# Attention with head mixing, then a leaky MLP: second mixing on array quarters, with a fixed order on every engine

## The chip, the cores and the metric

The kernel runs on one core of a Trainium2 chip. The metric is the time on the device in microseconds, as the median of several runs. TensorE (PE) multiplies matrices into PSUM; VectorE (DVE) and ScalarE (ACT) empty PSUM and work elementwise; GpSimd (POOL) works on SBUF alone; SyncE (SP) issues nearly all transfers.

## The reference

Four batches, twelve heads, 448 positions, head size 64. The scores of the twelve heads are mixed with one another before the softmax (first mixing) and after it (second mixing). The MLP has 1,792 tokens, width 768 and hidden width 2,048.

```python
scores = scale * np.matmul(q, k.transpose(0, 1, 3, 2))
scores = np.einsum('bhij,hg->bgij', scores, w_pre)       # first mixing
scores = scores - np.max(scores, axis=-1, keepdims=True)
attn = np.exp(scores)
attn = attn / (np.sum(attn, axis=-1, keepdims=True) + 1e-09)
attn = np.einsum('bhij,hg->bgij', attn, w_post)          # second mixing
attn_out = np.matmul(attn, v)
x = attn_out.transpose(0, 2, 1, 3).reshape(B * S, H * D)
h = x @ w_in
return np.maximum(0.01 * h, h) @ w_out
```

## The kernel before

The attention goes through the query rows in chunks: 120, 120, 120 and 88 rows of each batch, 16 chunks in all (`NCK`). The work of a chunk falls into three **units** (index `s`), each of up to 40 query rows (two "quads" of 20 rows, index `u`). A chunk of 88 rows is padded to 100, so its last unit has one quad. There are 48 units, and a full one makes four tiles of exponentials.

`scores(n, a)` multiplies q and k for head pair `a` of chunk `n` into two PSUM banks `pss` of pool `ps_x`; ScalarE or VectorE scales them into `st` (rows of the chunk on partitions). `regroup` is a transfer that collects ten rows of all twelve heads, 120 partitions, into a tile `r`. `softmax(n, s, u)` does the first mixing: eight 64x64 products of `r` and the constant `kpre` into two banks `psm` (pools `ps_m`). VectorE then takes the row maxima (`stat`), ScalarE the exponentials (`et`) with their sums, and after a unit's last quad VectorE makes `kp`, the weights of the second mixing divided by the sums. `mix(n, s, c)` does the second mixing for 128 keys `c`: here `et` is the stationary operand, `kp` the moving one, so the result `psa` (pool `ps_a`, two buffers of one bank) has the keys on partitions. It is copied to `at`, or to `half` for the last 64 keys. `values` multiplies `at` with `vt` (and `half` with `vend`) into `psx`, which shares the pool `ps_x` with the scores, and VectorE copies the result to `xo`, which is stored.

Beside this the MLP's weights are narrowed from 64-bit floats in 64 pieces: `Narrow` loads a piece (`craw`), `spread` casts it on ScalarE (`z`, `w`), `assemble` has three operations on VectorE (`top`, `exp`), `join` two on GpSimd and a store. In the last two chunks `prep_x` begins to prepare the attention's output for the MLP: sums of blocks, then each block as a high and a low part (`xh` by ScalarE, `xl` by VectorE).

The order of most matmuls is that of the program (`pin`); most copies, reductions and transfers before the change are placed by a scheduler. The loop has steps: in each chunk twelve of them (`SLOTS`), in every step one `mix`, in some a `softmax` of the next unit and a pair of `scores` of one of the next two chunks. `values` follows a unit's last `mix`. The MLP behind it is not touched.

Of the kernel before, what the change touches and what calls it, by code (L numbers as in the profile page):

```python
# [24 lines left out]
RUN = 2  # L25
# [8 lines left out]
def kernel(  # L34
# [50 lines left out]
    class Narrow:  # L85
# [7 lines left out]
        def __init__(self, pool, f, j, w=None):  # L93
            at = slice(PIECE * j, PIECE * (j + 1))
            self.pool, self.w, self.dst = pool, w, w_dram[f][:, at]
            self.raw = pool.tile([P, PIECE, 2], U32, tag="raw", name="craw", bufs=4)
            nc.sync.dma_start(self.raw.rearrange("p n w -> p (n w)"), w_moe[f, :, at].bitcast(U32))

        def spread(self, pin=lambda ins: ins):
# [3 lines left out]
            self.z = self.pool.tile([P, PIECE], F32, tag="z", name="z")  # L103
# [15 lines left out]
        def join(self, pin=lambda ins: ins):  # L119
# [3 lines left out]
            nc.sync.dma_start(self.dst, w)  # L123
# [11 lines left out]
    ps_a = pool("ps_a", 2, space=PSUM)  # L135
# [17 lines left out]
    def load_k(b, a):  # L153
        t = k_t[b, a] = p_k.tile([P, S], F32, tag="k", name="kt")
        for e in range(2):
            up = slice(D * e, D * (e + 1))
            nc.sync.dma_start(t[up], k[b, up, 2 * a + e, :])
# [4 lines left out]
    def load_q(n, *queues):  # L162
# [3 lines left out]
        for e in range(2):  # L166
            up = slice(D * e, D * (e + 1))
            (queues or (nc.sync, nc.sync))[e].dma_start(t[up, :, :m], src[up, :, e])
# [7 lines left out]
    def load_v(b, s):  # L176
        t = p_v.tile([P, NJ - 1, RUN, 2, D], F32, tag=f"v{s}", name=f"vt{s}")
        at = 2 * RUN * s
        nc.sync.dma_start(t.rearrange("p c a e d -> p c (a e) d"), v[b][:, :NJ - 1, at:at + 2 * RUN])
        for e in range(2):  # L180
            up = slice(HP * e, HP * (e + 1))
            nc.sync.dma_start(v_end[up, RUN * s:RUN * (s + 1), e], v[b][up, NJ - 1, at + e:at + 2 * RUN:2])
        v_t[b, s] = t

    def scores(n, a, banks=(ps_x, "x")):
        b, m = chunks[n][0], width(n)
# [9 lines left out]
        for e, ps in enumerate(two):  # L196
            to = s_t[n][:m, 2 * a + e, :]
            if e and (a % 2 or not n):
                nc.vector.tensor_scalar_mul(to, ps[:m, :S], scale)
            else:  # L200
                nc.scalar.activation(to, ps[:m, :S], AF.Copy, scale=scale)  # L201

    last_dma = [None]
# [4 lines left out]
    def regroup(n, a, z, *queues):  # L208
        m = width(n)
        for g in range(a, min(z, m // ROWS)):  # L210
            r_t[n, g] = t = r_all[turn[0] % SLOTS]
            turn[0] += 1
            last_dma[0] = (queues or (nc.sync, nc.sync))[g % 2].dma_start(
                t[LOW:LOW + RH], s_t[n][g:m:m // ROWS]
            )

    def softmax(n, s, u):
# [12 lines left out]
        for y, ps in enumerate(banks):  # L230
            g = 2 * u + y
            e = p_e.tile([P, S], F32, tag="e", name="et")
            es.append(e)
            nc.vector.tensor_reduce(st[:, 0, g:g + 1], ps[:, :S], axis=AX.X, op=ALU.max, negate=True)  # L234
            nc.scalar.activation(  # L235
                e, ps[:, :S], AF.Exp, bias=st[:, 0, g:g + 1], accum_out=st[:, 1, g:g + 1]
            )
        if u < len(sg) - 1:
            return
        kp = p_st.tile([P, NJ, H, ROWS], F32, tag="kp", name="kp")  # L240
# [3 lines left out]
        nc.vector.tensor_scalar_add(rs, st[:, 1, :z], 1e-9)  # L244
        nc.vector.reciprocal(rs, rs)
        nc.vector.tensor_mul(  # L246
            kp[:, :z].rearrange("p g h x -> p g (h x)"),
            kpost.rearrange("p h x -> p (h x)").unsqueeze(1).broadcast_to([P, z, H * ROWS]),
            rs.unsqueeze(2).broadcast_to([P, z, H * ROWS]),
        )  # L250

    def mix(n, s, c):

        sg = chunks[n][3][s]
        if s == 0 and c == 0:
            at_t[n] = (  # L260
                p_at.tile([P, NJ - 1, H, CHUNK], F32, tag="at", name="at"),
                p_at.tile([P, NPAIR, CHUNK], F32, tag="half", name="half"),
            )
        es, kp = e_t[n, s][0], kp_t[n, s]
        ps = ps_a.tile([P, 512], F32, tag="a", name="psa")
        if c < NJ - 1:
            at, nh, halves = at_t[n][0][:, c], H, ((0, P, 0, 1),)
        else:
            at, nh, halves = at_t[n][1], NPAIR, ((0, HP, 0, 2), (HP, HP, 1, 2))
        w = QUAD * len(sg)  # L270
        to = ps[:, :nh * w].rearrange("p (h u b y r) -> p u y h b r", h=nh, b=2, y=2, r=ROWS // 2)
        for g, e in enumerate(es):
            for p0, np, h, step in halves:
                mm(
                    to[p0:p0 + np, g // 2, g % 2], e[:, c * P:c * P + np],
                    kp[:, g, h::step].rearrange("p h (b r) -> p h b r", b=2), start=True, stop=True,
                )
        copy = nc.scalar.copy if n == NCK - 1 or c % 2 and (s * NJ + c) >= HALF - 1 else nc.vector.tensor_copy
        copy(at[:, :, QUAD * sg[0]:QUAD * sg[0] + w], ps[:, :nh * w].rearrange("p (h w) -> p h w", h=nh))  # L279

    def values(n, s):
        b, m = chunks[n][0], width(n)
        at, half = at_t[n]
# [4 lines left out]
        for a in range(RUN):  # L288
            for c in range(NJ - 1):
                for e in range(2):  # L290
                    mm(
                        ps[D * e:D * (e + 1), a, :m], w[:, c, a, e], at[:, c, 2 * (RUN * s + a) + e, :m],
                        start=a == c == 0, stop=False, skip_group_check=True,
                    )
        for a in range(RUN):
            mm(
                ps[:, a, :m], v_end[:, RUN * s + a].rearrange("p e d -> p (e d)"), half[:, RUN * s + a, :m],
                start=False, stop=a == RUN - 1, skip_group_check=True,
            )
        nc.vector.tensor_copy(  # L300
            xo_t[n][:, RUN * s:RUN * (s + 1), :m].rearrange("p a (x g) -> p a g x", x=ROWS),
            ps[:, :RUN, :m].rearrange("p a (g x) -> p a g x", x=ROWS),
        )
# [591 lines left out]
```

## Time and profile before

| | us |
|---|---|
| median of three runs (876.22 to 882.21) | 876.81 |
| profiled execution, its time | 873.24 |
| profiled execution, its span | 871.5 |
| attention, from the first scores to the first projections of the MLP | about 7 to 458 |

Times within the span are counted from its first instruction. The trace gives two rows for every float32 matmul of the program, and for each a weight load. Durations of consecutive matmuls overlap, so that their pace is read from their starts.

### The profile page before, as it was taken

How to read it: one execution, taken by the hardware profiler on the slowest of the kernel's cores; microseconds unless marked ns; L12 is line 12 of the kernel's file. 1: busy time of each engine (PE TensorE's matmuls, PEld its weight loads, DVE VectorE, ACT ScalarE, POOL GpSimd, SP SyncE). 2: the span in 40 equal slices, each digit the busy share in tenths (PEclk: the TensorE clock that was granted, in tenths of full speed). 3: DMA queues.
4: the chain of work that ended last, by engine and by line, in shares of the span. 5: the costliest groups of instructions: out<-in, count | busy, mean ns of one | idle time of the engine just before them, and what ended most of it. 6: DMA issues, size and time to landing. Idle time of an engine off the chain costs nothing.

```text
span 871.5 us, 17821 instructions
## 1 busy us (share of the span) xinstructions
PE 845.0 (97%) x6712; PEld 669.2 (77%) x6712; DVE 658.4 (76%) x1178; ACT 501.0 (57%) x1044; POOL 136.4 (16%) x154
## 2 busy tenths in 40 slices
PE   7999999999999999999999999999999999999998
PEld 3566666676666666667679999899989999999997
DVE  5688777887778877888897888688797555488565
ACT  2677666666666665666665554455764554454543
POOL 2043333323333232332200000000000000000000
PEclk9999999999999999999999999999999999999999
DMA  7888776997769877585637778536665121133343
GB/s 186 235 255 264 244 231 200 268 253 229 252 201 275 256 241 229 189 259 196 191 93 270 244 252 271 172 109 193 199 206 168 55 64 47 37 107 128 119 128 117
DMA packets 117126, 166.29 MB, mean 191 GB/s; under 512 B 37852, under 2 KB 100656, under 8 KB 117040
## 3 DMA queue, kind: packets, MB, share of 16 engines
q1 hardware_dynamic: 116140, 164.41, 61.2%
q8 instruction: 53, 0.87, 0.4%
q10 hardware_dynamic: 804, 0.73, 0.3%
q14 instruction: 33, 0.27, 0.1%
q0 software_dynamic: 96, 0.01, 0.0%
HBM read 92.91 MB, written 32.64 MB: 144 GB/s over the span
## 4 chain that ended last, share of the span: by engine, by line
PE 66%; DVE 5%; DMA 3%; ACT 2%; issue 1%; SPq 1%; DVEq 0%; ACTq 0%
PE pso L149 38%; PE psa L149 8%; PE psh L149 7%; PE pss L149 5%; PE psx L149 4%; PE psm L149 4%; DMA r<-st 1%; DVE xl L355 1%; DMA qt<-in_q 1%; DMA s_dram<-so 1%; DVE stat L234 1%; ACT et L235 1%; ACT xh L354 1%; DVE xo L300 0%; DVE kp L246 0%
## 5 line engine op out<-in xcount | busy, mean ns | idle before, releaser
L149 PEld LDWEIGHTS psa<-kp,et 128*128 128x128 f32 (+1 forms) x1840 | 157.5, 171 | 71.7 <-ACT st L201 24.0
L149 PE MATMUL psa<-kp,et 128*128 128x120 f32 (+1 forms) x1840 | 177.7, 260 | 3.9 <-DVE kp L246 2.8
L235 ACT ACTIVATE et<-psm,stat 128x448 f32<-128x448 f32 x184 | 115.7, 632 | 69.6 <-DVE stat L234 69.1
L149 PE MATMUL pso<-gh,wl 128*128 128x448 f32 x336 | 123.4, 367 | 1.3 <-ACT gh L354 1.3
L149 PE MATMUL pso<-gl,wh 128*128 128x448 f32 x336 | 123.6, 368 | 0.9 <-DVE gl L355 0.9
L149 PE MATMUL pso<-gh,wh 128*128 128x448 f32 x336 | 123.3, 367 | 0.0
L234 DVE TENSOR_REDUCE stat<-psm 128x1 f32<-128x448 f32 x184 | 106.4, 616 | 17.2 <-PE psm L149 16.9
L149 PE MATMUL pss<-kt,qt 64*64 64x448 f32 (+2 forms) x768 | 104.5, 558 | 6.5 <-DVE xo L300 4.4
L201 ACT ACTIVATE st<-pss 120x448 f32<-120x448 f32 (+1 forms) x141 | 71.9, 544 | 63.0 <-PE pss L149 63.0
L121 POOL TENSOR_TENSOR w<-w,exp 128x384 f32<-128x384 f32 x64 | 65.2, 1018 | 272.5 <-issue 100.0
L149 PE MATMUL psm<-r,kpre 64*64 64x448 f32 (+1 forms) x736 | 99.0, 547 | 6.7 <-DMA r<-st 6.7
L354 ACT CAST wh<-wo 128x768 fp32r<-128x768 f32 x56 | 46.8, 836 | 91.7 <-PE pso L149 86.9
L355 DVE TENSOR_TENSOR wl<-wo,wh 128x768 fp32r<-128x768 f32 x56 | 53.6, 958 | 45.8 <-ACT wh L354 42.2
L279 DVE COPY at<-psa 128x480 f32<-128x480 f32 (+1 forms) x105 | 66.3, 636 | 17.7 <-PE psa L149 17.7
L149 PEld LDWEIGHTS psm<-r,kpre 64*64 64x64 f32 (+1 forms) x736 | 31.9, 135 | 49.4 <-issue 37.0
L149 PEld LDWEIGHTS pso<-gh,wl 128*128 128x128 f32 x336 | 63.6, 189 | 6.7 <-ACT gh L354 1.7
L149 PEld LDWEIGHTS pso<-gl,wh 128*128 128x128 f32 x336 | 63.6, 189 | 6.5 <-DVE gl L355 1.5
L149 PEld LDWEIGHTS pso<-gh,wh 128*128 128x128 f32 x336 | 63.6, 189 | 5.0
L149 PE MATMUL psx<-at,vt 128*64 128x120 f32 (+1 forms) x1152 | 65.4, 263 | 0.5 <-DVE xo L300 0.5
L122 POOL TENSOR_TENSOR w<-w,top 128x384 f32<-128x384 f32 x64 | 64.3, 1004 | 5.0
L355 DVE TENSOR_TENSOR gl<-g,gh 128x896 fp32r<-128x896 f32 x56 | 60.7, 1084 | 1.9 <-ACT gh L354 1.9
L149 PEld LDWEIGHTS psx<-at,vt 128*64 128x64 f32 x1152 | 56.9, 137 | 1.6 <-DVE xo L300 0.7
(117 smaller groups left out, 1415.6 us busy)
## 6 DMA issues: line engine op xcount, KB each, us to landing
r<-st SPq DMA_DIRECT2D x182, 210.0 KB
craw<-in_w_moe SPq DMA_DIRECT2D x64, 384.0 KB
w_dram<-w SPq DMA_DIRECT2D x64, 192.0 KB
wi<-w_dram SPq DMA_DIRECT2D x32, 384.0 KB
wo<-s_dram SPq DMA_DIRECT2D x64, 192.0 KB
wo<-w_dram SPq DMA_DIRECT2D x48, 192.0 KB
xr<-x_dram SPq DMA_DIRECT2D x33, 224.0 KB
so<-w_dram SPq DMA_DIRECT2D x16, 384.0 KB
```

The lines of the kernel that those rows point to most:

```text
L121: pin(nc.gpsimd.tensor_mul(w, w, self.exp.bitcast(F32)))
L122: pin(nc.gpsimd.tensor_add(w, w, self.top.bitcast(F32)))
L149: pin(nc.tensor.matmul(*args, **kw))
L201: nc.scalar.activation(to, ps[:m, :S], AF.Copy, scale=scale)
L234: nc.vector.tensor_reduce(st[:, 0, g:g + 1], ps[:, :S], axis=AX.X, op=ALU.max, negate=True)
L235: nc.scalar.activation(e, ps[:, :S], AF.Exp, bias=st[:, 0, g:g + 1], accum_out=st[:, 1, g:g + 1])
L279: copy(at[:, :, QUAD * sg[0]:QUAD * sg[0] + w], ps[:, :nh * w].rearrange("p (h w) -> p h w", h=nh))
L354: hold(nc.scalar.copy(hi, raw))
L355: hold(nc.vector.tensor_sub(lo, raw, hi.bitcast(F32)))
```

## The change

It rewrites the attention's loop and leaves the MLP's alone.

- The second mixing (`second_mix`) works on 64x64 quarters of the array: 64 rows of `et` (half `b` of the query rows) by 64 keys (half `ch`), with `kp` of 60 columns, or 30 for the last 64 keys. The two row halves go to different banks. A unit's mixing is in two parts of two key blocks each; `ps_a` has one buffer of two banks instead of two of one. One copy empties both banks: VectorE for part 0 (960 elements a partition), ScalarE for part 1 (720). `half` is now a piece of `at`, and `kp` and `kpost` have half the columns.
- Scores are made two chunks ahead: those of chunk `n + 2` in chunk `n`, two pairs in every unit; all pairs of the chunks 0 and 1 come ahead of the loop. The last two chunks have none.
- Every instruction of the attention is pinned to the program's order on its engine, the transfers on SP too. A unit runs: regroup of the next chunk's unit, narrowing load, first mixing of the next unit's quad 0, a score pair, part 0, first mixing of quad 1, a score pair, part 1, `weights` (`kp`), `values` of the chunk before. `join` and `spread` of the narrowing stand at fixed places, a piece in four half units of five (before: one in 8/3 steps, with four steps to a unit).
- Copies out of scores: three of four by ScalarE in every unit. `xo` is copied in two instructions.
- The preparation of x is divided into `join_x` (sums, in the loop on GpSimd) and `split_x`. In the last two chunks part 1 goes through the banks of `ps_x`.

```diff
-    ps_a = pool("ps_a", 2, space=PSUM)
+    ps_a = pool("ps_a", 1, space=PSUM)
...
+    def second_mix(n, s, part, *copies):
         sg = chunks[n][3][s]
...
+        if len(copies) == 1:
+            ps = ps_a.tile([P, 2, 512], F32, tag="a", name="psa")
+            banks = [ps[:, 0], ps[:, 1]]
         else:
...
+            banks = [ps_x.tile([P, 512], F32, tag="x", name="psa") for _ in range(2)]
+        w = ROWS * len(sg)
+        at0 = 0
+        for c in (2 * part, 2 * part + 1):
+            whole = c < NJ - 1
+            nh = H if whole else NPAIR
+            for g, e in enumerate(es):
+                for b in range(2):
+                    for ch in range(2):
+                        up, to = slice(HP * b, HP * (b + 1)), slice(HP * ch, HP * (ch + 1))
+                        keys = slice(c * P + HP * ch * whole, c * P + HP * ch * whole + HP)
+                        out = banks[b][to, at0 * w:(at0 + nh) * w].rearrange(
+                            "p (h g r) -> p g h r", h=nh, r=ROWS // 2
+                        )
+                        weight = kp[up, g] if whole else kp[up, g, ch::2]
+                        mm(out[:, g], e[up, keys], weight, start=True, stop=True)
+            at0 += nh
...
+    for a in range(NPAIR):
+        copy = scores(1, a)
+        copy(0, nc.scalar)
+        copy(1, nc.vector)
...
+        if more:
+            if us > 0:
+                exp = first_mix(*nxt, 0)
+                exp(0)
+            copy = scores(n + 2, 2 * s)
+            copy(0, nc.scalar)
+            if us > 0:
+                exp(1)
+            copy(1, nc.vector)
+            join(2 * i)
+            second_mix(n, s, 0, nc.vector.tensor_copy)
+            spread(2 * i)
+            narrow_load(2 * i + 1)
+            if us > 1:
+                exp = first_mix(*nxt, 1)
+            copy = scores(n + 2, 2 * s + 1)
+            copy(0, nc.scalar)
+            if us > 1:
+                exp(0)
+                exp(1)
+            copy(1, nc.scalar)
+            second_mix(n, s, 1, nc.scalar.copy)
+            join(2 * i + 1)
+            spread(2 * i + 1)
+            if nxt:
+                weights(*nxt)
+            if n:
+                values(n - 1, s)()
```

TensorE before, one unit in the middle of the attention (`x8` counts matmuls of the program; `psa` is the second mixing, `psm` the first, `pss` scores, `psx` values):

```order
L149 MATMUL psx<-at,vt_2043 64x120 x12
L149 MATMUL psx<-half,vend 128x120 x2
L149 MATMUL psa<-kp,et 128x12x2x5 x4
L149 MATMUL pss<-kt,qt 64x448 x2
L149 MATMUL pss<-kt,qt 36x448 x2
L149 MATMUL psm<-r_139,kpre 64x448 x2
L149 MATMUL psm<-r_140,kpre 64x448 x2
L149 MATMUL psa<-kp,et 128x12x2x5 x8
L149 MATMUL pss<-kt,qt 64x448 x2
L149 MATMUL pss<-kt,qt 36x448 x2
L149 MATMUL psm<-r_141,kpre 64x448 x2
L149 MATMUL psm<-r_142,kpre 64x448 x2
```

TensorE now, one unit at about the same place:

```order
L153 MATMUL psm<-r_137,kpre 64x448 x2
L153 MATMUL psm<-r_138,kpre 64x448 x2
L153 MATMUL pss<-kt,qt 64x448 x2
L153 MATMUL pss<-kt,qt 56x448 x2
L153 MATMUL psa<-kp,et 64x12x5 x32
L153 MATMUL psm<-r_139,kpre 64x448 x2
L153 MATMUL psm<-r_140,kpre 64x448 x2
L153 MATMUL pss<-kt,qt 64x448 x2
L153 MATMUL pss<-kt,qt 56x448 x2
L153 MATMUL psa<-kp,et 64x12x5 x16
L153 MATMUL psa<-kp,et 64x6x5 x16
```

The mixing's twelve wide and eight narrow matmuls are 64 small ones now, in two groups, each behind a score pair; the values stand behind the second.

VectorE before, from one `kp` to the next (`top`, `exp`: narrowing; `stat<-psm`: maxima):

```order
L246 TENSOR_TENSOR kp<-kpost,stat 128x480
L199 TENSOR_SCALAR st<-pss 120x448
L111 TENSOR_SCALAR top<-z 128x384
L114 SCALAR_TENSOR_TENSOR top<-z,top 128x384
L234 TENSOR_REDUCE stat<-psm 128x1 x2
L117 TENSOR_SCALAR exp<-top 128x384
L279 COPY half<-psa 128x6x40
L300 COPY xo<-psx 128x2x12x10
L279 COPY at<-psa 128x12x40
```

VectorE now, the unit up to `kp` and `xo`:

```order
L237 TENSOR_REDUCE stat<-psm 128x1 x2
L206 TENSOR_SCALAR st<-pss 100x448
L113 TENSOR_SCALAR top<-z 128x384
L116 SCALAR_TENSOR_TENSOR top<-z,top 128x384
L119 TENSOR_SCALAR exp<-top 128x384
L293 COPY at<-psa 128x2x24x20
L237 TENSOR_REDUCE stat<-psm 128x1 x2
L113 TENSOR_SCALAR top<-z 128x384
L116 SCALAR_TENSOR_TENSOR top<-z,top 128x384
L119 TENSOR_SCALAR exp<-top 128x384
L255 TENSOR_SCALAR stat<-stat 128x4
L256 RECIPROCAL stat<-stat 128x4
```

The copy of the mixing's first part now stands behind two reductions, a score copy and a narrowing piece, in every unit alike; `kp` and the two copies of `xo` follow the last row shown.

## Rows read from the trace of the kernel before

**Rows 1.** The page: busy time by engine, the chain that ended last, the exponentials.
```profile
PE 845.0 (97%) x6712; PEld 669.2 (77%) x6712; DVE 658.4 (76%) x1178; ACT 501.0 (57%) x1044; POOL 136.4 (16%) x154
...
PE 66%; DVE 5%; DMA 3%; ACT 2%; issue 1%; SPq 1%; DVEq 0%; ACTq 0%
...
L235 ACT ACTIVATE et<-psm,stat 128x448 f32<-128x448 f32 x184 | 115.7, 632 | 69.6 <-DVE stat L234 69.1
```

**Rows 2.** Windows, all engines: length, busy time of each, granted clock, DMA share, GB/s.
```profile
60.00:180.00 120.00, 118.17 (x1306) 79.66 (x1305) 96.61 (x216) 79.18 (x204) 41.53 (x43) 1.00 0.80 241
180.00:300.00 120.00, 116.95 (x1293) 78.19 (x1296) 95.71 (x213) 78.70 (x202) 41.37 (x42) 1.00 0.81 242
...
420.00:460.00 40.00, 36.55 (x408) 29.66 (x405) 36.20 (x72) 24.88 (x58) 2.56 (x2) 1.00 0.45 132
```

**Rows 3.** Timeline of TensorE over one unit: start, length, work.
```profile
211.52 0.68 PE L149 MATMUL psa<-kp,et 128*64 128x60 f32 x16
212.03 1.41 PE L149 MATMUL psx<-at,vt 128*64 128x120 f32 x24
...
213.91 1.06 PE L149 MATMUL psa<-kp,et 128*128 128x120 f32 x8
214.89 0.98 PE L149 MATMUL pss<-kt,qt 64*64 64x448 f32 x8
215.69 0.93 PE L149 MATMUL psm<-r,kpre 64*64 64x448 f32 x8
216.55 2.04 PE L149 MATMUL psa<-kp,et 128*128 128x120 f32 x16
218.53 0.98 PE L149 MATMUL pss<-kt,qt 64*64 64x448 f32 x8
219.33 0.93 PE L149 MATMUL psm<-r,kpre 64*64 64x448 f32 x8
220.19 0.68 PE L149 MATMUL psa<-kp,et 128*64 128x60 f32 x16
220.70 1.41 PE L149 MATMUL psx<-at,vt 128*64 128x120 f32 x24
```

**Rows 4.** Window of the tile psx alone, columns as before without ACT and POOL.
```profile
60.00:414.00 354.00, 77.84 (x1093) 66.72 (x1092) 22.44 (x40) 1.00 0.77 236
```

**Rows 5.** TensorE's groups by form, 60 to 415 us: count, busy, mean ns.
```profile
L149 PE MATMUL psm<-r,kpre 64*64 64x448 f32 x304 | 79.2, 538 | 1.9 <-DMA r<-st 1.9
```

**Rows 6.** Timeline of VectorE in the same stretch.
```profile
207.88 0.36 DVE L117 TENSOR_SCALAR exp<-top 128x384 uint32<-128x384 uint32 x1
208.16 1.15 DVE L234 TENSOR_REDUCE stat<-psm 128x1 f32<-128x448 f32 x2
...
211.06 0.66 DVE L246 TENSOR_TENSOR kp<-kpost,stat 128x480 f32<-128x480 f32 x1
211.63 0.62 DVE L199 TENSOR_SCALAR st<-pss 120x448 f32<-120x448 f32 x1
212.17 1.14 DVE L234 TENSOR_REDUCE stat<-psm 128x1 f32<-128x448 f32 x2
214.10 0.58 DVE L300 COPY xo<-psx 128x240 f32<-128x240 f32 x1 [0.79 <-PE psx L149]
214.53 0.35 DVE L111 TENSOR_SCALAR top<-z 128x384 uint32<-128x384 uint32 x1
214.91 0.56 DVE L114 SCALAR_TENSOR_TENSOR top<-z,top 128x384 uint32<-128x384 uint32 x1
215.39 0.65 DVE L279 COPY at<-psa 128x480 f32<-128x480 f32 x1
```

**Rows 7.** Windows of ten microseconds with the most traffic.
```profile
80.00:90.00 10.00, 10.00 (x113) 6.62 (x107) 8.98 (x20) 6.10 (x15) 2.94 (x4) 1.00 0.95 276
160.00:170.00 10.00, 10.00 (x113) 6.46 (x105) 8.51 (x20) 6.58 (x17) 4.01 (x4) 1.00 1.02 288
```

**Rows 8.** Timeline of TensorE at the start: the first mixing of all.
```profile
17.16 3.71 PE L149 MATMUL psm<-r,kpre 64*64 64x448 f32 x16 [4.63 <-DMA r<-st]
```

More of the change, by code (lines that the diff above doesn't have):

```diff
@@ L252, in mix @@
-    def mix(n, s, c):
+            kpost.rearrange("p h x -> p (h x)").unsqueeze(1).broadcast_to([P, z, RH // 2]),
+            rs.unsqueeze(2).broadcast_to([P, z, RH // 2]),
+        ))
+    def second_mix(n, s, part, *copies):
         sg = chunks[n][3][s]
[L259 to L267, printed above, removed]
-        else:
[L269 to L279, printed above, removed]
@@ L666 @@
     for u in range(2):
-        softmax(0, 0, u)
-    scores(1, 0)
-    scores(1, 1, (ps_a, "a"))
-    def step(n, s, c):
-        mix(n, s, c)
-        if c < NJ - 1 or not n:
-            return
-        values(n - 1, s)
-        if n % NB == 0:
-            load_v(chunks[n][0], s)
-    pieces = [(f, j) for f in range(NF) for j in range(4)]
-    begun = {8 * i // 3: piece for i, piece in enumerate(pieces)}
-    narrowing, late = {0: Narrow(p_c, *begun[0])}, None
-    for n in range(NCK):
-        b = chunks[n][0]
-        if n == NCK - 1:
+        exp = first_mix(0, 0, u)
@@ new lines, in join, with tail @@
+    def join(at):
+        if at - 4 in narrowing:
+            narrowing[at - 4].assemble(pin)
+            narrowing[at - 4].join(pin)
+    parts = [(c, k) for c in range(HC) for k in range(X_PARTS)]
+    def tail(add=nc.gpsimd):
+        c, k = parts.pop(0)
+        split_x(c, k)
+        if parts:
+            join_x(*parts[0], add)
+        if c + 1 < HC and k in (2, 3, 5):
+            load_raw(0, c + 1, (2, 3, 5).index(k))
+        if c and k == 0:
+            load_raw(0, c, 3)
+    for i, (n, s) in enumerate(units):
+        b, last = chunks[n][0], n == NCK - 1
+        nxt = units[i + 1] if i + 1 < len(units) else None
+        us = len(chunks[nxt[0]][3][nxt[1]]) if nxt else 0
+        more = n + 2 < NCK
+        if last and s == 0:
@@ new lines @@
+        for u in range(us):
+            exp = first_mix(*nxt, u)
+            exp(0)
+            exp(1)
+        if last and s == 1:
+            mixed.close()
+            open_hidden()
+            prep_wi(0, "a", pin)
+        values(n - 1, s)()
+        join(2 * i)
+        spread(2 * i)
+        if i > 3 * NCK - 6:
+            tail()
+        if i == 3 * NCK - 1:
+            tail()
+        second_mix(n, s, 0, nc.scalar.copy)
+        if last and s == 1:
+            prep_wi(0, "s", pin)
@@ L752 @@
+        narrow_load(2 * i + 1)
+        if nxt:
+            weights(*nxt)
+        if i > 3 * NCK - 6:
+            tail()
+        join(2 * i + 1)
+        spread(2 * i + 1)
+        second_mix(n, s, 1, nc.vector.tensor_copy, nc.scalar.copy)
+        if last and s == 1:
+            prep_wi(0, "b", pin)
+        tail()
+        if last and s == 0:
+            load_wi(0, 0)
     store_x(NCK - 2)
@@ L754 @@
     for s in range(3):
[L755 to L757 removed]
+        values(NCK - 1, s)()
+        for _ in range((2, 1, 1)[s]):
+            tail(nc.vector)
     store_x(NCK - 1)
```

229 lines of the change are left out of this document (108 added, 121 removed).

## The prediction

> **What bounds the kernel now.** I read the page first, then the windows, then one unit of TensorE's timeline. The page puts TensorE at 97% busy and two thirds of the chain that ended last on it [rows 1]. That share hides two programs: up to about 460 us attention, after it the MLP, which the change leaves alone; only the first can move. In the attention windows TensorE is busy nearly throughout at granted clock 1.00 (the 2.4 GHz level), VectorE 80%, the DMA engines 80% at 241 GB/s [rows 2]. So TensorE is first, and two others stand close behind it.
>
> One unit (one third of a chunk, forty query rows in twelve heads) is the period to work with. In the timeline the reader is to subtract starts, since the durations of pipelined matmuls overlap. From one psx start (212.03) to the next (220.70) are 8.67 us, and no row between them has an idle gap [rows 3]: TensorE sets this unit. It splits into values 1.88, two score pairs 0.80 each, two first mixings 0.86 each, together 5.20, and the second mixing (psa): 0.98 + 1.98 for the 128-row tiles and 0.51 for the half tile, together 3.47. A matmul of the program shows as two records. On average a unit takes longer: 1,093 psx records at 28 a unit are 39 units in 354 us, 9.07 us each [rows 4]; 0.4 us and more is waiting.
>
> **The second mixing.** Removed per full unit: 24 records of 128x128 with 120 columns and 16 of 128x64 with 60. Added: 64 matmuls, 128 records, each on a 64x64 quarter, 96 with 60 columns and 32 with 30. What a record costs in that form no row shows, so it is bounded. Upper bound: the half tile's records, 0.51/16 = 32 ns each [rows 3], taken as a cost of every record: 128 x 32 = 4.1 us, more than the 3.47 it replaces. Lower bound: the same rows read as pairs. Two column halves run side by side, so a pair takes 64 ns; if the two row halves run side by side as well, four records take 64 ns: 32 x 64 = 2.04 us. For that speaks the first mixing: it is made of 64x64 quarters already, its records last 0.54 us each [rows 5], yet eight of them pass in 0.86 us [rows 3], which is two rounds of four. What it doesn't show is four weight loads every 64 ns, because there each load has some 0.4 us to hide in. I take 2.04 us, since shape and bank layout (each row half in a bank of its own) are those of the first mixing. TensorE's unit falls by 1.43 to 7.24 us.
>
> The trace speaks against one rule here. In it, records of the half tile pass every 32 ns and those of the first mixing in rounds of four. The Trainium skill (TensorE: Matmul & The Clock Gate, "Wait — 56ns, not 53.3ns?") says that start-to-start never drops below about 25 ns, however few columns; by it the mixing would take an estimated 128 x 25 = 3.2 us and the gain would nearly vanish. Nothing in this trace has small quarters back to back, so it stands as a rival below.
>
> **What else the engines get.** VectorE loses half of the kp product (480 to 240 elements: from 0.57 us, the spacing 211.06 to 211.63, to about 0.3) and some of the evacuation; xo becomes two copies (bounds: the present 0.58 and twice that; I take 0.6) [rows 6]. ScalarE takes three of the four score copies and 720 of 1,680 evacuated columns. Neither is late by sum. By order it is another matter: ps_a now has one buffer of two banks, so the second half of the mixing waits for VectorE's copy of the first half. Behind it on TensorE's queue stand the values and the next unit's first mixing. From the start of the first mixing, VectorE's way to that copy is: matmuls 0.93, two reductions 2 x 0.53, score copy 0.54, three narrowing operations 0.38 + 0.48 + 0.28, a copy of 960 elements at the rate of 480 in 0.57, so about 1.07, and its end 0.09 [rows 3, 6]: 4.8 us. TensorE is there after 0.86 + 0.80 + 1.02 + 0.86 + 0.80 = 4.3. So TensorE stalls 0.5 us in the four units in five that have a narrowing piece in that place, and 7.24 becomes about 7.6, or 7.45 over all units, the short ones included. Without a piece VectorE is there at 3.7 and the stall is gone. The wait for xo at the second score bank is covered: 0.5 to 0.6 us of copy beside the 0.86 us first mixing that TensorE does meanwhile.
>
> **Transfers.** Bytes stay as they are. 241 GB/s x 9.07 us are 2.19 MB a unit. The busiest stretches of ten microseconds reach 276 GB/s at share 0.95 and 288 at 1.02 [rows 7]. At 282 a unit can't take under 7.8 us. This is above the 7.45 of the engines: while weights are narrowed, the transfers are next. Narrowing is also pulled from 42 units into 40, which adds about 0.06 MB, 0.2 us at most. The regroup transfers get about two units of lead, so I cost their latency at nothing; that cover goes if the queue falls behind by a unit. Squeezed between 7.45 and 8.0 I take 7.8. SP's issues (0.8 us or less for each of four regroups a unit) fit.
>
> **Front and end.** All six score pairs of the second chunk now come ahead of the first mixing, which today starts at 17.16 us after an idle gap of 4.63 [rows 8]. With two banks each pair waits for its copies (0.8 + 0.6 or so): about 9 us, of which 4.6 fall into the gap, so 4 us late. The same pairs are missing from the last units. There VectorE is the bound, 36.2 of 40 us [rows 2]; it loses copies to ScalarE and the sums of x to GpSimd, which I value at 4 us over six units (bounds 0 and 9). Front and end cancel.
>
> **Sum.** 40 units x (9.07 − 7.8) = 51 us. The profiled execution took 873.2 us, the median is 876.8, 3.6 more: 873.2 − 51 + 3.6 = 826 us.
>
> **Rivals.**
> *The engines' order decides, not the transfers* (part of the forecast): unit 7.45, 40 x 1.62 = 65, 812 us; without the stall on VectorE 7.05 and 796.
> *Records leave one by one.* The quarters overlap, but the queue lets no record go sooner than some floor between the 16 and the 32 ns of the bounds. At the middle, 24 ns, the mixing takes 3.1 us, TensorE 8.3 in a full unit, and with small waits a unit is 8.3 on average: 40 x 0.77 = 31 us gained, 846. For it: no row shows small records faster than 32 ns. Against: the rounds of four, which start together. It would show as equal steps in the psa rows. By the floor of the section named above the time would be an estimated 850.
> *Fixed queues pass waits on.* Casts of raw weights stand on ScalarE ahead of score copies and exponentials; if a load comes late, everything behind waits, where today's queues are mixed more freely. If that eats half the gain, unit 8.45: 40 x 0.62 = 25, 855 us. If it eats all, the edit does nothing that counts: 870 to 880. For it: transfers near their ceiling. Against: one and a half units between load and cast, 11 us.
> *Slower: the record price of 32 ns holds.* Then the mixing takes 4.1, TensorE 9.28 in a full unit, and with 46 full units' worth (184 exponentials by four [rows 1]) x 0.61 = 28 us the time is 905. It decides from 27 ns a record (3.47/128) on. For it: the only small records in the trace have that pace, and their weight loads could be what sets it. Against: those run in pairs, so the pair's 64 ns is what one load costs, and quarters in different rows load different rows.
>
> **How the numbers follow.** Chances: forecast with the engines' variant 0.65 (796 to 838), records one by one 0.08 (846), waits eat half 0.12 (840 to 860), no change 0.05, slower 0.10. A change within 1% is about what measurement here can't tell from none. Faster 0.84, same 0.06, slower 0.10. The range of 800 to 862 takes in the forecast, the records that leave one by one and the half-eaten case; what stays outside is no change, slower and the best end.
>
> **What would show it.** Right: in the timeline psa drops from 3.47 to about 2 us a unit, period of psx near 7.8, DMA share above 0.9 while narrowing lasts, and a gap ahead of the second psa group that names VectorE's at copy. If psa takes 3 us or over, the quarter price was wrong. If psa takes 2 and the period stays over 8.4, a queue is the cause, and the waits view names it: a raw-weight transfer under ScalarE's cast, or xo under the scores. Wrong as well if the MLP, 460 us on, changes length, since nothing there was counted.

## The result, and the profile after

The changed kernel takes 864.37 us (863.1 to 868.02, four runs), the kernel before 877.08 us beside it: ratio 0.985, 95% interval [0.9802, 0.9898]. It is 12.7 us faster where 51 were forecast; the whole interval lies below 1, the gain is under 2%. 826 us and the range up to 862 were wrong, the direction was right. The profiled execution took 863.1 us, with a span of 861.4 us.

The page, its first line and the row of the queue that brings instructions: TensorE's busy time fell by 49 us and VectorE's is as before, against [rows 1]. Instruction packets number 85; before there were 53.

```profile
PE 795.6 (92%) x10760; PEld 634.0 (74%) x10760; DVE 654.5 (76%) x1147; ACT 502.5 (58%) x1023; POOL 148.0 (17%) x164
...
q8 instruction: 85, 1.39, 0.7%
```

Windows of all engines, columns as in [rows 2]. In the attention TensorE now idles 11 to 12% of the time, VectorE is at 84% where it was at 80%, and the transfers moved from 241 GB/s to 260.

```profile
60.00:180.00 120.00, 106.16 (x2574) 73.68 (x2567) 102.64 (x218) 83.62 (x207) 44.20 (x45) 0.99 0.86 261
180.00:300.00 120.00, 107.10 (x2436) 73.25 (x2429) 99.44 (x213) 81.81 (x202) 44.91 (x46) 0.96 0.85 258
```

Window of the tile psx alone, as in [rows 4]. It counts 1064/28 = 38 units in 328 us: 8.63 us a unit, where 7.8 was forecast. From psx to psx the same 38 units took 343.4 us before (58.0 to 401.4, 9.04 each) and take 328.1 us now (60.3 to 388.4, 8.63 each).

```profile
60.00:388.00 328.00, 81.17 (x1064) 68.02 (x1064) 21.19 (x76) 0.98 0.83 256
```

TensorE's timeline over one unit with nothing late in it, the answer to [rows 3]; the last three rows belong to the unit behind it.

```profile
127.13 1.45 PE L153 MATMUL psx<-at,vt 128*64 128x120 f32 x24
...
129.15 0.98 PE L153 MATMUL psm<-r,kpre 64*64 64x448 f32 x8
129.95 0.96 PE L153 MATMUL pss<-kt,qt 64*64 64x448 f32 x8
130.70 1.13 PE L153 MATMUL psa<-kp,et 64*64 64x60 f32 x64
131.63 0.96 PE L153 MATMUL psm<-r,kpre 64*64 64x448 f32 x8
132.39 0.96 PE L153 MATMUL pss<-kt,qt 64*64 64x448 f32 x8
134.27 1.13 PE L153 MATMUL psa<-kp,et 64*64 64x60 f32 x64 [0.92 <-DVE at L293]
135.33 1.25 PE L153 MATMUL psx<-at,vt 128*64 128x100 f32 x24
...
137.93 1.37 PE L153 MATMUL pss<-kt,qt 64*64 64x448 f32 x5
...
139.11 0.57 PE L153 MATMUL pss<-kt,qt 64*64 64x448 f32 x3
...
142.75 1.13 PE L153 MATMUL psa<-kp,et 64*64 64x60 f32 x64 [0.63 <-DVE at L293]
```

From psx to psx this unit takes 135.33 − 127.13 = 8.20 us. The first half of the mixing takes 131.63 − 130.70 = 0.93 us, the second 135.33 − 134.27 = 1.06 us, together 1.99 where [rows 3] had 3.47. Ahead of the second half TensorE idles 0.92 us, and the releaser is VectorE's copy of the first half. VectorE in the same stretch, the answer to [rows 6], and GpSimd beside it:

```profile
128.84 0.41 DVE L257 TENSOR_TENSOR kp<-kpost,stat 128x240 f32<-128x240 f32 x1
129.26 0.58 DVE L323 COPY xo<-psx 128x120 f32<-128x120 f32 x2
130.21 1.16 DVE L237 TENSOR_REDUCE stat<-psm 128x1 f32<-128x448 f32 x2 [0.37 <-PE psm L153]
131.28 0.62 DVE L206 TENSOR_SCALAR st<-pss 120x448 f32<-120x448 f32 x1
131.81 0.35 DVE L113 TENSOR_SCALAR top<-z 128x384 uint32<-128x384 uint32 x1
132.20 0.56 DVE L116 SCALAR_TENSOR_TENSOR top<-z,top 128x384 uint32<-128x384 uint32 x1
132.79 0.36 DVE L119 TENSOR_SCALAR exp<-top 128x384 uint32<-128x384 uint32 x1
133.07 1.15 DVE L293 COPY at<-psa 128x960 f32<-128x960 f32 x1
...
137.06 1.08 DVE L257 TENSOR_TENSOR kp<-kpost,stat 128x240 f32<-128x240 f32 x1
138.07 0.50 DVE L323 COPY xo<-psx 128x100 f32<-128x100 f32 x2
```

```profile
136.87 1.01 POOL L123 TENSOR_TENSOR w<-w,exp 128x384 f32<-128x384 f32 x1 [1.51 <-ACT st L208]
```

From the first mixing (129.15) to the end of the copy (134.22) are 5.07 us, nothing idle on VectorE's way but the wait for the matmuls; TensorE's part follows 0.05 us later. The unit is therefore 5.12 from psm to the mixing's second half + 1.06 + 2.02 of values (127.13 to 129.15) = 8.20 us, and VectorE sets it. The next unit takes 8.49 (135.33 to 143.82): kp takes 1.08 us, not 0.41, while GpSimd's product runs from 136.87 to 137.88 beside it. The copies of xo begin only at 138.07, the last records of the score pair, which share a pool with psx, only at 139.11, and the wait for the at copy is there again (the row at 142.75). Over the loop (60 to 388 us) this copy is TensorE's longest wait ahead of matmuls; the second longest is for its own instructions (`issue`):

```profile
PE psa L153 <- DVE at L293: 24.4, 30, 1.4
PE psa L153 <- issue: 5.7, 8, 1.2
```

Such `issue` waits add up to 7.8 us ahead of all matmuls in this window; before the change there were none of them. One of 1.19 us ended at 257.45 us, and in the stretch behind it TensorE's granted clock is 0.52; the unit that begins at 258.02 takes 10.62 us:

```profile
257.00:264.00 7.00, 6.55 (x55) 4.42 (x59) 2.10 (x7) 2.30 (x7) 0.00 (x0) 0.52 0.91 264
```

So TensorE was relieved as forecast, and an ordinary unit is held by something else at 8.2 us and more. Two places outside the units also lost time. At the start, TensorE's timeline and a window, to be held against [rows 8]:

```profile
17.44 0.98 PE L153 MATMUL pss<-kt,qt 64*64 64x448 f32 x8 [2.91 <-ACT st L208]
...
21.60 1.88 PE L153 MATMUL pss<-kt,qt 64*64 64x448 f32 x8 [0.65 <-ACT st L208]
24.12 1.88 PE L153 MATMUL pss<-kt,qt 64*64 64x448 f32 x8 [0.65 <-ACT st L208]
...
28.19 4.56 PE L153 MATMUL psm<-r,kpre 64*64 64x448 f32 x21
```

```profile
19.00:31.00 12.00, 9.98 (x48) 3.05 (x48) 3.54 (x7) 2.44 (x6) 0.00 (x0) 0.50 0.66 187
```

The first mixing starts at 28.19 us instead of 17.16: six score pairs stand ahead of it. From 19 us on they follow each other every 2.53 us, at a granted clock of 0.50, that is the 1.2 GHz level, after an idle gap of 2.91 us. The first psx of all comes 2.3 us late (60.3 for 58.0). At the end, from unit 41 to the MLP's first matmul of its steady part, it takes 60.3 us instead of 56.6. TensorE, ScalarE and SyncE there:

```profile
405.05 1.81 PE L153 MATMUL psa<-kp,et 64*64 64x60 f32 x58 [4.10 <-DVE xo L323]
```

```profile
401.07 0.56 ACT L376 CAST xh<-xr 128x448 fp32r<-128x448 f32 x1 [4.33 <-DMA xr<-x_dram]
```

```profile
391.15 0.58 SPq L329 DMA_DIRECT2D x_dram<-xo  x1
...
397.37 2.48 SPq L361 DMA_DIRECT2D xr<-x_dram  x4
```

ScalarE stands 4.33 us before a block of x that SyncE issues only at 397.37, behind a store issued at 391.15, four regroups and a store of weights; what ScalarE and VectorE do next comes late, and TensorE idles 4.10 us. In sum the loop gives −15.3 us, the start +2.3, the end +3.7: −9.3 of the 10.1 by which the spans differ. The MLP is as long as before within a microsecond.

### The profile page after: what moved, and what is told of

Same layout as the page of the kernel before. It is cut to its first block, busy times and chain, and to the rows that moved or that the text cites. A ratio compares the mean times of both kernels' runs of the same rounds, so it can differ in the third digit from the quotient of the medians.

```text
span 861.4 us, 26026 instructions
## 1 busy us (share of the span) xinstructions
PE 795.6 (92%) x10760; PEld 634.0 (74%) x10760; DVE 654.5 (76%) x1147; ACT 502.5 (58%) x1023; POOL 148.0 (17%) x164
## 4 chain that ended last, share of the span: by engine, by line
PE 48%; DVE 4%; DMA 3%; issue 2%; ACT 2%; POOL 0%; SPq 0%; ACTq 0%; POOLq 0%; DVEq 0%
PE pso L153 37%; PE psh L153 7%; PE psx L153 2%; PE psa L153 1%; DMA wi<-w_dram 1%; PE psm L153 1%; ACT et L243 1%; DMA wo<-w_dram 1%; DVE xl L377 0%; DVE stat L237 0%; DMA xr<-x_dram 0%; DMA w_dram<-w 0%; DVE at L293 0%; ACT xh L376 0%; DMA x_dram<-xo 0%
## 5 line engine op out<-in xcount | busy, mean ns | idle before, releaser
L153 PEld LDWEIGHTS psa<-kp,et 64*64 64x64 f32 x5888 | 112.0, 137 | 90.4 <-DVE at L293 57.5
L153 PE MATMUL psa<-kp,et 64*64 64x60 f32 (+1 forms) x5888 | 120.1, 221 | 42.7 <-DVE at L293 26.5
L153 PE MATMUL pss<-kt,qt 64*64 64x448 f32 (+2 forms) x768 | 115.7, 566 | 10.6 <-ACT st L208 9.3
L208 ACT ACTIVATE st<-pss 120x448 f32<-120x448 f32 (+1 forms) x138 | 74.6, 543 | 41.3 <-PE pss L153 33.9
L153 PE MATMUL psm<-r,kpre 64*64 64x448 f32 x736 | 96.0, 573 | 0.7 <-DMA r<-st 0.7
L153 PEld LDWEIGHTS pss<-kt,qt 64*64 64x64 f32 (+2 forms) x768 | 40.8, 130 | 64.8 <-ACT st L208 26.6
L153 PE MATMUL psx<-at,vt 128*64 128x120 f32 (+1 forms) x1152 | 72.3, 277 | 5.2 <-DVE at L296 4.3
L153 PEld LDWEIGHTS psx<-at,vt 128*64 128x64 f32 x1152 | 61.1, 144 | 12.1 <-DVE at L296 5.1
L377 DVE TENSOR_TENSOR gl<-g,gh 128x896 fp32r<-128x896 f32 x56 | 60.8, 1086 | 1.9 <-ACT gh L376 1.9
L376 ACT CAST gh<-g 128x896 fp32r<-128x896 f32 x56 | 52.6, 939 | 0.6 <-PE psh L153 0.6
```

The costliest lines, as they stand in the source:

```text
L153: pin(nc.tensor.matmul(*args, **kw))
L208: pin(nc.scalar.activation(to, ps[:m, :S], AF.Copy, scale=scale))
L376: hold(nc.scalar.copy(hi, raw))
L377: hold(nc.vector.tensor_sub(lo, raw, hi.bitcast(F32)))
```

## The experiments

Four theories. **A**: the fixed order on the engines, VectorE's above all, sets the unit. **B**: the transfers set it, at a lower rate than assumed. **C**: not their rate, but the place of the loads in SyncE's one queue. **D**, formed last: VectorE's path and the transfers are two limits close together, each hidden behind the other. Times are medians, ratios are to the kernel before, run beside it.

| | us | ratio, interval |
|---|---|---|
| changed kernel | 864.37 | 0.985 [0.9802, 0.9898] |
| e1_copy_first | 887.51 | 1.0164 [1.009, 1.0238] |
| e2_no_gpsimd | 862.22 | 0.9863 [0.9802, 0.9923] |
| e3_three_st | 864.45 | 0.9877 [0.9838, 0.9916] |
| e4_front_banks | 867.14 | 0.9907 [0.9874, 0.9941] |
| e5_copy_first_two_tops | 874.12 | 0.9985 [0.995, 1.0021] |
| e6_piece_behind_xo | 861.4 | 0.9848 [0.9809, 0.9886] |
| e7_front_q_early | 859.3 | 0.9839 [0.9789, 0.9889] |
| e8_tail | 861.44 | 0.9829 [0.9775, 0.9883] |
| e9_all | 853.83 | 0.9715 [0.9661, 0.977] |
| e10_no_assemble | 853.43 | 0.972 [0.9663, 0.9778] |
| e11_quarters_old_order | 920.71 | 1.0482 [1.0422, 1.0543] |
| e12_more_traffic | 934.85 | 1.0645 [1.0563, 1.0726] |
| e13_half_loads | 854.81 | 0.9758 [0.9694, 0.9822] |
| e14_all_half_loads | 842.65 | 0.9622 [0.9566, 0.9678] |
| e15_half_loads_no_assemble | 826.12 | 0.9436 [0.9389, 0.9483] |
| e16_all_loads_by_gpsimd | 861.92 | 0.9839 [0.9797, 0.9881] |
| e17_all_no_assemble | 847.89 | 0.9675 [0.9643, 0.9707] |
| e18_no_loads_no_assemble | 811.61 | 0.9251 [0.9199, 0.9302] |

**VectorE's order: e1, e5, e6.** e1 puts the narrowing piece behind the copy of the first half; e5 adds a second buffer for `top` and `exp`, paid for with one buffer of exponentials; e6 is e5 with the second piece of a unit moved behind xo.

```diff
+            second_mix(n, s, 0, nc.vector.tensor_copy)
             join(2 * i)
-            second_mix(n, s, 0, nc.vector.tensor_copy)
...
+            self.top = top = self.pool.tile([P, PIECE], U32, tag="top", name="top", bufs=2)
...
             values(n - 1, s)()
+            join(2 * i + 1)
```

> Theory A: with one psa buffer, the way of a unit leads over VectorE: maxima, score copy, narrowing piece (1.26 us), copy of the mixing's first part, then TensorE's second part and the values. With the narrowing piece behind the copy, four of five units lose up to 1.2 us of it; the next limit is TensorE at 7.3 us or VectorE at 7.0. Expected 825 to 845 us, the gap ahead of the second psa group gone. Theory B, transfers hold the unit at 8.2 to 8.6 us: no change beyond 3 us, 861 to 867. Theory C, the wait only moves behind the second maxima: 855 to 864.

> As e1 (copy of the mixing's first part ahead of the narrowing piece), and top and exp with two buffers each. Theory A2: e1's loss of 23 us came from VectorE waiting for GpSimd (30.5 us in its waits) between two pieces that now follow each other within 2.4 us, so that xo came late and the score bank with it (25.5 us). With that wait gone the units of 7.1 us that e1 already shows become the rule: 835 to 850 us. Rival: kp and xo stay behind two pieces and two maxima, the score bank still waits in most units: 860 to 885.

> As e5, and the second narrowing piece stands behind xo. Theory A2 with the score bank as the second loop: xo is no longer late, both loops through VectorE are as short as they get, units of 7.1 to 7.6 us: 820 to 840 us. Theory B, transfers: at share 0.86 and 261 GB/s nothing more is to be had, 855 to 865 whatever the order. Rival D, VectorE is full (6.9 us of 7.1): the second piece delays the next maxima, units of 7.8 to 8.0: 840 to 852.

e1 is slower by 23 us than the changed kernel, which none of its three forecasts had. Its waits, 60 to 388 us (total, times, longest):

```profile
DVE top L113 <- POOL w L124: 28.1, 22, 2.3
...
PE pss L153 <- DVE xo L323: 23.7, 13, 2.2
```

VectorE now waits for GpSimd to give `top` back, and the scores for xo. Units of 7.06 to 7.1 us turn up, but beside units of 9.4 to 12.3. The second buffer takes back more than half of the loss (e5, 874.12, as its rival said; its trace isn't read here). e6 gains nothing clear. So VectorE's order matters, and no order tried gives what A hoped for.

**GpSimd beside VectorE: e2.** GpSimd's two narrowing operations are left out.

```diff
-            pin(nc.gpsimd.tensor_mul(w, w, self.exp.bitcast(F32)))
-            pin(nc.gpsimd.tensor_add(w, w, self.top.bitcast(F32)))
```

> Leaves out GpSimd's two operations of every narrowing piece, so the MLP's weights are wrong. Theory: the kp product takes 1.05 us beside GpSimd and 0.40 alone, and xo, queued behind it, holds the second score bank. Then kp falls to 0.40 everywhere and the time by 5 to 15 us, to 850 to 860. Rival: the copy of the mixing's first part sets the unit anyway; kp falls, the time stays within 3 us of 864.

The kp products by form, 60 to 388 us, in the changed kernel and in e2:

```profile
L257 DVE TENSOR_TENSOR kp<-kpost,stat 128x240 f32<-128x240 f32 x35 | 33.0, 943 | 1.2
```

```profile
L255 DVE TENSOR_TENSOR kp<-kpost,stat 128x240 f32<-128x240 f32 x36 | 14.7, 408 | 1.2
```

kp falls from 943 to 408 ns, 18 us of VectorE's busy time in all, and the kernel's time stays (862.22, as the rival said): a cheaper instruction on the engine that looked like the limit brings nothing that can be measured.

**A third score tile: e3.** `st` gets a third buffer, paid for with one buffer less of q and of exponentials.

```diff
+            s_t[n] = (p_s3 if n % 3 == 2 else p_s).tile([CHUNK, H, S], F32, tag="s", name="st")
```

> A third st buffer (place for it from one q buffer, one et buffer and the exp tile). Theory: at the start of each of the fourteen chunks the first score copies wait for the regroup transfers of the chunk two before, 1 to 3 us, and TensorE's clock falls behind some of these gaps: 8 to 15 us gained, 849 to 856. Rival: the regroup is as late for the first mixing as for the copy, so the wait moves to TensorE: within 3 us of 864.

Nothing: 864.45, as the rival said. As far as this run tells, which gave up two other buffers, the score copies' waits for the regroups aren't what holds the unit.

**Start and end: e4, e7, e8, e9.** e4 spreads the early pairs over the mixing's banks too, e7 also loads q(2) ahead of the regroups, e8 issues the load of x first and gives the sums of x back to VectorE, e9 is e6, e7 and e8 together.

```diff
-        copy = scores(1, a)
+        copy = scores(1, a, ((ps_x, "x"), (ps_m[a // 3], "m"))[a % 3 > 0])
...
+    load_q(2)
     for s in range(3):
         regroup(0, s, *((nc.sync, nc.scalar), ())[s > 0])
-    load_q(2)
...
-    def tail(add=nc.gpsimd):
+    def tail(add=nc.vector):
```

> The six score pairs of chunk 1 ahead of the loop go through six banks in place of two. Theory: they take 0.9 us a pair in place of 2.5, the first mixing starts at 20 to 22 us in place of 28.2, the time falls by 5 to 7 us to 857 to 860. Rival: units 0 to 2, which have no values, catch up as they did (first values 2.3 us late where the first mixing was 11 late), so under 2 us are gained.

> e4 with q of chunk 2 loaded ahead of the first regroups. Theory: in e4 the 4.7 us won ahead of the first mixing were lost to scores of chunk 2, which waited 3.1 us for q, queued behind ten regroups, and ran at half clock after it. With q early the first values start at 54 to 57 in place of 60.3: 858 to 861 us. Rival: the transfers of k, v and r are next and take it all: 863 to 866.

> The first loads of x stand ahead of the last chunk but one's store and regroups, and the sums of x are VectorE's again. Theory: in the last six units ScalarE's casts wait for x (4.3 us once) and for GpSimd's sums (1.6 to 3.6 us a time), and the evacuations behind them hold TensorE, 12 us of gaps in all: 854 to 860 us. Rival: VectorE, with 2 us of sums more, is the bound as in the kernel before: 862 to 868.

> e6, e7 and e8 in one kernel. If the three sizes add (3, 5 and 3 us): 852 to 856 us. If the front's and the end's gains were noise: 859 to 864.

In e4 the first mixing starts at 23.5 us, 4.7 earlier, but the first psx at 60.8, no earlier: a 3.1 us wait for q(2) takes its place, and nothing is gained. With q(2) moved (e7) it starts at 22.0 and the first psx comes at 59.3. e6, e7 and e8 alone are 3 to 5 us under the changed kernel, too little to be told from it; the three together are 10.5 under it: 853.83, with a ratio of 0.9715 to the kernel before, faster than both and within what was expected.

**Less on VectorE: e10.** The three narrowing operations on VectorE are left out of the changed kernel.

```diff
-            self.top = top = self.pool.tile([P, PIECE], U32, tag="top", name="top")
...
+            self.top = self.exp = self.z
```

> The changed kernel without VectorE's three operations of every narrowing piece (the weights are wrong); casts, GpSimd's work and every transfer stay. Theory V: VectorE's own load, 7.6 us in a unit with two pieces, and its place on the way to the mixing's second part hold the unit; with 2 x 1.25 us gone TensorE is the limit, 7.1 to 7.3 us a unit: 64 pieces x 0.6 to 1.0 us, 805 to 830 us. Theory B, transfers: unit stays above 8 us, 855 to 864.

VectorE's busy time in 60 to 180 us falls from 102.64 to 73.34 us, and the time by 11 us only, between what the two theories forecast; the transfers stay at 261 GB/s.

**Quarters without the order: e11.** The kernel before, with `second_mix` and the narrow `kp` in place of `mix`, called at the old steps.

```diff
+        if c % 2 == 0:
+            return
+        part = c // 2
+        copies = (nc.scalar.copy if part or n == NCK - 1 else nc.vector.tensor_copy,)
```

> The kernel before with the quarter mixing alone: two parts a unit, one double bank, half kp, xo in two copies; loop, scheduler and front stay. If the fixed order lost the gain: 835 to 850 us. If VectorE is the limit in either order: 860 to 872. If the order is what gained the 1.5%: 875 or more.

Slower than the kernel before (879.98 beside it) by 41 us, more than any forecast had. The psx window has 812/28 = 29 units in 290 us, 10 us each; behind it the wait of TensorE's that is the longest (60 to 430 us):

```profile
60.00:350.00 290.00, 64.76 (x812) 54.99 (x812) 16.34 (x58) 0.96 0.70 218
```

```profile
PE psa L149 <- DVE at L286: 61.5, 33, 2.4
```

With one pair of banks for the mixing TensorE waits for VectorE's copy in this order too. From here the changed kernel, with its fixed order and the scores two chunks ahead, is 56 us away.

**More traffic: e12.** A load of 192 KB more in every half unit, 15.7 MB in all.

```diff
+        if at < 80:
+            f, j = pieces[at % len(pieces)]
+            pin(nc.sync.dma_start(extra, w_moe[f, :, PIECE * j:PIECE * (j + 1)].bitcast(U32)[:, :PIECE]))
```

> The changed kernel with a further load of 192 KB in every one of the first 80 half units, 15.7 MB or 16% more traffic in the loop. Theory B, transfers hold the unit: 40 units x 1.2 us, 905 to 915 us. Theory V: the transfers have room, 864 to 875.

```profile
60.00:350.00 290.00, 73.64 (x804) 62.19 (x806) 15.76 (x56) 0.89 0.84 257
```

The time rises by 70 us, 20 more than B had at the most, and the rate doesn't (257 GB/s). That spoke for B, with a reserve: SyncE also waited 49.8 us for its own last extra load, since all go to one tile, and the granted clock fell to 0.89.

**Less traffic: e13, e14, e15, and e16 to e18.** In e13 every second load of expert weights is left out (that piece is narrowed from the first one). e14 is e9 with this, e15 is e14 with e10's cut as well. e17 is e9 with e10's cut alone, e18 is e15 with all loads but the first left out. e16 is e9 with the loads issued by GpSimd, which also moves them from a hardware queue to a software one (25.18 MB on q0 in its page).

```diff
+            if first[0] is not None and (4 * f + j) % 2:
+                self.raw = first[0]
+                return
...
+                nc.gpsimd.dma_start(self.raw.rearrange("p n w -> p (n w)"), w_moe[f, :, at].bitcast(U32))
```

> The changed kernel, with every second load of the expert weights left out (that piece is narrowed again from the first piece loaded, so half of the narrowed weights are wrong; every engine does the same work): 12.4 MB less, 0.31 MB a unit. Theory B (transfers at about 260 GB/s are the limit): 0.31 / 0.26 = 1.2 us off a unit, 8.63 to 7.4-7.6, and 40 units make 40 to 46 us: 818 to 825, at a rate still near 255 or a share that begins to fall. Theory A (the engines' order and waits set the unit, the transfers follow): under 10 us, 855 to 864, at 225 GB/s. Theory C (SyncE's queue): in between, 840 to 855, since an issue of 0.4 to 0.6 us and its wait go with each load.

> e9_all with the same loads left out (half of the narrowed weights wrong). B: 853.8 less 35 to 46 us, 808 to 819. A: 845 to 854.

> e9_all with half of the loads and also VectorE's three narrowing instructions left out (all narrowed weights wrong). B: with transfers out of the way VectorE is next, so that what was worth nothing in e10 is worth something here: 5 to 15 us under e14, units of 7.1 to 7.4 us, near TensorE's own busy time, 800 to 808. A: 835 to 850, and no more than e10 gave (a few us) under e14.

> e9_all with the loads of the expert weights issued by GpSimd, bytes and work unchanged. B: 850 to 862, the same rate of 255 to 267 GB/s in the middle. C: loads no longer stand behind the regroups in SyncE's queue, so the rate rises over 270 GB/s and 38 units of 8.2 instead of 8.5 us give 840 to 845.

> e9_all with VectorE's three narrowing instructions left out and every load in place (all narrowed weights wrong). Theory D (two limits close together: VectorE's path at 8.2 us a unit, the transfers at 8.4): the transfers still hold it at 8.3 to 8.4 us a unit, 845 to 850, 4 to 9 under e9, so that the two steps together (e15, 27 us under e9) are worth more than 11 and 4 to 9 added up. VectorE alone: 832 to 838, since then the loads add only e14's 11 us to e15.

> e15 with all loads of expert weights but the first left out (all narrowed weights wrong; 12.4 MB less again). D and transfers that still count in the long units of e15 (14, 10, 11, 9.6 us where the rest are 7.1): these shrink, mean unit 7.85 to 7.2-7.4, 802 to 812. If the long units at every twelfth place come from the change of the batch (new keys and values in a burst) and not from the mean rate, they stay and it gives 818 to 826.

B alone fell: about a seventh of the traffic gone (12.4 MB of 40 units at 2.25) gave 10 and 11 us (e13, e14), where 40 and 35 us at the least were expected, and the transfers simply slowed to 225 and 235 GB/s. But the two cuts together (e15) gave 28 us, between what A and B expected. e17 closed the square, at 847.89, within what D expected. The psx windows of e9, e17 (less on VectorE), e14 (less traffic) and e15 (both), in this order:

```profile
60.00:350.00 290.00, 71.70 (x953) 59.94 (x952) 19.20 (x68) 0.98 0.85 260
```

```profile
60.00:350.00 290.00, 73.12 (x955) 60.62 (x954) 19.89 (x70) 0.98 0.88 265
```

```profile
60.00:350.00 290.00, 72.00 (x980) 60.00 (x980) 19.66 (x70) 1.00 0.75 235
```

```profile
60.00:350.00 290.00, 79.12 (x1036) 66.41 (x1036) 21.00 (x74) 0.98 0.79 246
```

A count of records in a window is good to a part of a unit only, so the length of a unit is better taken from the starts in TensorE's timeline, first psx to the 39th: 8.53 us in e9 (57.60 to 381.56), 8.38 with VectorE relieved (56.88 to 375.21), 8.25 with the transfers relieved (53.36 to 366.86), 7.85 with both (53.66 to 352.02), and 7.52 in e18 with nearly no loads left (54.91 to 340.56). Each cut by itself meets the other limit. In times: 5.9 us for the one, 11.2 for the other, 27.7 for both. (By the ratios, which compare with the runs of before beside each: 3.5, 8.1 and 24.4 us; each carries some 5 us of uncertainty.) The single units show how: the median one takes 8.40 us in e9, 8.39 with the transfers relieved, 8.15 with VectorE relieved and 7.12 with both, the longest 12.6, 9.3, 12.7 and 14.1. So VectorE's way holds the ordinary unit, and the loads make others long.

Two reserves. TensorE's waits for its own instructions are in these numbers too, 7.0 us in e9, 11.3 in e17, 3.2 in e14 and 10.2 in e15, and nothing takes them out. And a load that is left out takes its bytes, its issue and its wait with it; that it is the rate of all transfers that counts is argued from e17 and e12, not shown. In e17 ScalarE waits for transfers, 60 to 375 us:

```profile
ACT w L107 <- DMA w_dram<-w: 17.8, 15, 2.2
...
ACT st L199 <- DMA r<-st: 14.2, 7, 4.4
```

And in e15 TensorE runs a full unit without waiting for an engine. From its timeline (no row left out has an idle gap):

```profile
93.49 1.45 PE L152 MATMUL psx<-at,vt 128*64 128x120 f32 x24
...
97.06 1.13 PE L152 MATMUL psa<-kp,et 64*64 64x60 f32 x64
...
99.50 0.87 PE L152 MATMUL psa<-kp,et 64*64 64x60 f32 x47
101.02 0.44 PE L152 MATMUL psa<-kp,et 64*64 64x30 f32 x17 [0.66 <-issue]
101.39 1.45 PE L152 MATMUL psx<-at,vt 128*64 128x120 f32 x24
```

101.39 − 93.49 − 0.66 (a wait for its own instructions) = 7.24 us, the unit that the forecast gave TensorE alone; the next one takes 7.09. e18, at 811.61, is within what D expected, but the long units of its rival stay too: 11.7 and 9.9 us where the values of a new batch begin. In the first of them the trace names the transfers: ScalarE's score copy waits 3.28 us for regroups, VectorE's 3.69 us for new keys, and TensorE's next score pair 2.96 us for the copy. No run took these away.

e16 speaks against C: with the loads away from SyncE's queue the time is 8 us longer than e9's, not 9 to 14 shorter, and 180 to 300 us run at 251 GB/s. It doesn't rule C out, since the software queue is another change. One thing that grew is TensorE's wait for its own instructions ahead of matmuls, from 7.0 us in e9 to 16.8 in the 38 units; why it grew stays open.

## Why the prediction was wrong

**Right: the price of the quarters.** 2.04 us a unit were forecast, 1.99 measured, and the 32 ns rival as well as the records that leave one by one are out: 64 records in 0.93 us are 14.5 ns each. In the trace four start within 20 to 30 ns and the next four 58 ns after the first. The Trainium skill (TensorE: Matmul & The Clock Gate, "Wait — 56ns, not 53.3ns?") has start-to-start never below about 25 ns; this trace goes below it, with matmuls on different quarters. TensorE's unit of 7.24 is what e15 shows.

**Wrong in size: VectorE's way.** The forecast took 4.8 us to the copy of the first half and 0.5 of stall: by its own terms 7.74 in a unit with a piece, 7.6 over the full units and 7.45 with the short ones. Measured in the unit shown: 5.12 and 0.92, the rest of the unit 1.06 + 2.02 where 1.02 + 1.88 was counted, so 8.20. Three steps are longer than the spacing they were taken from: the reductions begin 1.06 us after the first mixing (0.93 taken), the second narrowing operation takes 0.59 (0.48), the copy 1.15 (1.07). On the mean of 38 units, e13, the changed kernel with half of the loads, has 8.43 (59.55 to 379.87).

**Wrong: "the wait for xo is covered", and kp at 0.3.** kp is 0.41 alone and 1.08 beside GpSimd (mean 0.943 over 35). Then xo and the reductions are late and the unit takes 8.49. The Trainium skill (SBUF — State Buffer, "SBUF: two separate sides") says that a VectorE operation with two SBUF inputs and a GpSimd operation exclude each other for a whole instruction; the rows agree, as far as GpSimd's spans are exact: kp ends 0.26 us after GpSimd's product. By e2 it is worth no measurable time here.

**Wrong in size: transfers at 282 GB/s, 7.8 us a unit.** This is the term that the sum rests on. The two busiest windows of ten microseconds [rows 7] were taken as a rate that lasts. It doesn't: with VectorE relieved and all loads in place (e17) the transfers run at 265 GB/s over 290 us, and the unit is 8.38; e10, the same cut in the changed kernel's order, has 8.43 (60.24 to 380.42). In e9 and e12 the rate is 260 and 257. The bytes were about right: 2.19 and at most 0.06 MB for the narrowing pulled forward are 2.25, and at 265 GB/s these take 8.49 us. The forecast's own bytes at its own rate gave 7.98; it took 7.8.

**Wrong as a rule: the larger of two limits.** The forecast took the maximum of 7.45 and 7.8. In the changed kernel's order each limit alone allows 8.43 (e13, e10), and both together gave 8.63; in e9's they are 8.25 and 8.38, and both gave 8.53. So the maximum falls short by 0.20 and 0.15 us a unit even with the right sizes, since different units meet different limits. All in all that makes 38 x (8.63 − 7.8) = 32 of the 41 us of span that are missing: 24 for the size, 8 for the rule. The next point makes 6, and most of the rest is in the count: 40 units from 9.07 were forecast, 38 from 9.04 are what changed.

**Counted at nothing: TensorE's own instructions and its clock.** The 32 us hold 7.8 us of waits for instructions, in groups that the forecast let run through, and stretches at a lower clock behind some gaps (0.52 from 257 to 264 us); no run takes either out.

**Wrong: "front and end cancel".** They cost 2.3 + 3.7 = 6 us. The 4 us at the start were worked out at full clock; from 19 us on the pairs ran at the 1.2 GHz level, 2.53 us each. At the end SyncE's order put the load of x behind what waited. That this was avoidable, e9 shows with e6, e7 and e8 together; alone, the gains of e7 and e8 are too small to tell.

**The rivals.** "Fixed queues pass waits on" (chance 0.12) came nearest in time. It stated 855 us, but its own sum, 876.8 less 25, gives 852. It didn't come true by the mechanism it named: in the changed kernel's trace ScalarE is never idle ahead of one of the 64 casts of raw weights, and the waits of 60 to 388 us have neither of the two that were to show a queue, a raw load under the cast or xo under the scores; TensorE's longest is for VectorE's copy.

## What to carry to other kernels

Take no short burst as a lasting rate: look for the longest stretch in which the resource was the one waited for, and if there is none, give the estimate a wide lower side. When two resources stand within a few per cent of each other behind the bottleneck, forecast neither's value but something above both (here 0.15 to 0.20 us on 8.4), and expect that relieving either one will look useless; only the cut of both at once, and the square of four runs, shows what each is worth. Rewriting a start or an end for the loop's sake needs its own sum, at the clock that this stretch really gets.

## What the runs showed of the hardware

- Matmuls on four quarters of the array: 58 ns for four records of 64x64 with 60 columns, weights loaded for each, 14.5 ns each over 64.
- A product of two SBUF operands on VectorE (128x240, float32) took 0.41 us alone and up to 1.08 us in the loop beside a GpSimd product.
- The transfers of this mixture stayed at 256 to 265 GB/s over some 300 us in the changed kernel, e9, e12 and e17, whatever work the engines had, while 10 us windows before the change reached 276 and 288. That this rate is a ceiling is argued, not shown.
- With 10,760 matmul records instead of 6,712, and 85 instruction packets instead of 53, TensorE waits for its own instructions in the middle of a group (0.66 us at 101.02 in e15; 7.8 us from 60 to 388 in the changed kernel). Before there were no such gaps among its matmuls in the loop. The count of records alone doesn't set them: with half of the loads, e13 has 1.7 us.
- Behind idle gaps TensorE's granted clock fell to the 1.2 GHz level, 0.50 from 19 to 31 us and 0.52 from 257 to 264 us; the row of a score pair lasts 0.98 us at 17.44 and 1.88 at 21.60.
